# A planned three-stage kernel: attention in groups of three units, own maxima behind the scores

## The chip, the cores and the metric

The kernel runs on one core of one Trainium2 chip. The metric is the device time of one execution in microseconds; the time before is 989.42 us, the median of three runs (987.98, 989.42, 990.55).

## What is computed

Three stages, each on the output of the one before: an attention whose queries are averaged in twos, a dense feed-forward layer with ELU, and a soft mixture of experts. The change touches the first.

```python
def _attn_ref(q, k, v):                  # (4, 8, 1152, 64) each
    q_pool = q.reshape(B, H, S // 2, 2, D).mean(axis=3)
    scores = scale * np.matmul(q_pool, k.transpose(0, 1, 3, 2))
    scores = scores - np.max(scores, axis=-1, keepdims=True)
    attn = np.exp(scores)
    attn = attn / (np.sum(attn, axis=-1, keepdims=True) + 1e-09)
    return np.matmul(attn, v)

h = x @ w_in; g = np.where(h > 0, h, np.exp(np.minimum(h, 0)) - 1); x = g @ w_out
# then soft mixture of 8 experts with 4 slots each on the 2304 x 512 result
```

## The kernel before

**The attention.** The 32 heads are taken in 16 pairs. A pair has two halves of 288 pooled queries, and each half goes over nine chunks of 128 keys: 18 units a pair. A unit (`step`, L675) consists of the scores of both heads (`qk`, L688: eight matmuls of 288 columns, the two heads on the two halves of the array's rows), the exponential on ScalarE (L700), the running sum of P on GpSimd or DVE (L709), and P times V (`pv`, L695: two heads on the two halves of the array's columns). At the end of a half, the sums over the keys are formed on TensorE (`sums`, L719).

The row maximum must be known before a half begins, since its negative is added by the fourth product of `qk` (the operand `nm`). It is computed from single products of q and k (L619) and a reduction on DVE (L628). Six products of 384 columns per pair have a score tile of their own (`max_unit`, "own" maxima); eighteen of 192 columns are carried behind the scores of a unit of the pair before, in the free columns of the same tile (`carry`). `max_end` (L664, L668, L672) turns the maxima into a row.

q and k of a pair are transposed on TensorE (L580 for q, L603 for k: six blocks in a score tile and three in an accumulator), cast by ScalarE (L588, L610) and the rest of the cast is taken by a subtraction on DVE (L589, L611).

**Tiles.** Three score tiles of two PSUM banks each (psA twice, psS) serve scores, own maxima and transposes in turn; two accumulators (psC) serve P times V, sums, the row of the maxima and k's last three blocks. Six buffers hold P.

**What sets the order.** All operations are entered with a wished position, a duration and their operands, and a planner (`Plan.run`) lists them on the five engines by estimated times; the instructions are then issued in that order, engine by engine, and the semaphores follow from the tiles that they touch. TensorE's operations of the attention are fixed: they keep the order of their positions. Positions are written in groups of GU = 2 units (L569): scores of the group's units, then P times V of the group before.

```python
        t = TG(p, u // GU, 0.45 * (u % GU))
        t2 = TG(p, u // GU + 1, TC + 0.2 * (u % GU))
        ...
        if more:
            max_red(S_, *more, 1, NH, t + 0.02, [("SX", p, u)])
```

The last argument makes the planner put the reduction of a carried maximum behind the unit's exponential (`SX`).

The dense layer follows (L856, L895, 32 slots), with its weights decoded on DVE beside the attention and the layer itself, and the experts at the end (L1241, L1277), whose weights arrive as the buffers come free.

Of the kernel before, what the change touches and what calls it, by code (L numbers as in the profile page):

```python
# [270 lines left out]
DQ = [-10, 0.61]
DK = [[-9, 0.3], [-9, 0.3]]
UC = -14
MAX1 = [[-2, 0.4], [-2, 1.3], [0, -0.1], [0, 0.9], [1, -0.1], [1, 1.3]]
# [1112 lines left out]
```

## Time and profile before

| | |
|---|---|
| median of three runs | 989.42 us |
| span of the profiled execution | 990.1 us |
| TensorE matmuls busy | 955.2 us, 96% |
| VectorE busy | 757.0 us, 76% |
| ScalarE busy | 497.7 us, 50% |
| GpSimd busy | 396.2 us, 40% |
| mean granted clock of TensorE | 0.980 |
| chain that ended last | TensorE 85%, VectorE 8%, DMA 3% |

The profiled execution's span lies within the range of the three runs, 0.7 us above their median; there is no other time for it. The attention takes about the first half of the span, the dense layer the time up to some 908 us, the experts the rest. GpSimd is busy in the attention alone. A busy TensorE row includes its pipeline: consecutive rows overlap, so durations on TensorE are read from start to start.

### The profile page before, as it was taken

To read this page: it belongs to the slowest core of one execution; us is meant where nothing else is said; L and a number is where in the kernel's file an instruction comes from. 1 tells how busy PE (TensorE), PEld (TensorE's weight loads), DVE (VectorE), ACT (ScalarE), POOL (GpSimd) and SP (SyncE) were. 2 spreads that over 40 slices of the span, in tenths; PEclk is the share of its full clock that TensorE was granted. 3 is DMA by queue.
4 is the path that set the end of the run, shared out by engine and by line. 5 is a ranking of instruction groups with operands and counts; after the bars stand their busy time and mean duration, and the time that the engine had idled before them with its cause. 6 is when DMAs were issued, how large, how long until landed. Compare 5 with 4: busy or idle time off the path is not lost.

```text
span 990.1 us, 20893 instructions
## 1 busy us (share of the span) xinstructions
PE 955.2 (96%) x8474; PEld 782.5 (79%) x8474; DVE 757.0 (76%) x1278; ACT 497.7 (50%) x891; POOL 396.2 (40%) x278
## 2 busy tenths in 40 slices
PE   7999999999999999999999999999999999999885
PEld 4777767676777677677899999999999999998343
DVE  6677788888777778899998989998866877766213
ACT  2556566555665556565664444444434376442213
POOL 2878889798878878887400000000000000001000
PEclk7999999999999999999999999999999999999897
DMA  7133424224334322221263333333423023233999
GB/s 177 45 86 85 106 74 122 67 78 119 86 85 117 74 73 75 63 72 34 65 219 113 117 95 131 106 98 110 157 86 107 32 97 107 65 107 109 402 362 317
DMA packets 103663, 114.86 MB, mean 116 GB/s; under 512 B 43664, under 2 KB 74896, under 8 KB 103568
## 3 DMA queue, kind: packets, MB, share of 16 engines
q1 hardware_dynamic: 103568, 113.55, 37.7%
q8 instruction: 66, 1.08, 0.5%
q14 instruction: 29, 0.24, 0.1%
HBM read 100.27 MB, written 13.18 MB: 115 GB/s over the span
## 4 chain that ended last, share of the span: by engine, by line
PE 85%; DVE 8%; DMA 3%; ACT 1%; issue 1%; SPq 0%; ACTq 0%; DVEq 0%
PE psC L895 20%; PE psA L856 20%; PE psC L695 13%; PE psA L688 10%; PE psS L688 5%; PE psA L619 3%; PE psS L619 2%; DVE memf L628 2%; DMA memzq<-in_moe_w_dram 2%; PE psA L1241 2%; PE psC L719 1%; PE psA L603 1%; DMA memf<-memf 1%; PE psA L580 1%; PE psC L664 1%; PE psC L1277 1%
## 5 line engine op out<-in xcount | busy, mean ns | idle before, releaser
L709 POOL TENSOR_TENSOR memf<-memf 128x576 f32<-128x576 f32 x241 | 359.8, 1495 | 65.0 <-ACT memf L700 38.6
L895 PE MATMUL psC<-memz 128*128 128x288 f32 x1512 | 224.6, 296 | 1.2 <-DVE memf L906 0.7
L895 PEld LDWEIGHTS psC<-memz 128*128 128x128 f32 x1512 | 208.1, 188 | 4.6 <-ACT memf L514 1.6
L695 PE MATMUL psC<-memf 128*64 128x288 f32 x1152 | 174.6, 420 | 0.0
L700 ACT ACTIVATE memf<-psA 128x576 f32<-128x576 f32 x206 | 132.8, 651 | 66.8 <-PE psA L619 57.7
L628 DVE TENSOR_REDUCE memf<-psA 128x2 f32<-128x384 f32 (+3 forms) x235 | 142.4, 617 | 28.7 <-PE psA L619 13.9
L1347 POOL MEMSET memf<- 128x2048 f32 x1 | 1.8, 1817 | 387.8 <-DVE memz L517 387.8
L906 DVE TENSOR_TENSOR memf<-psC,memf 128x288 f32<-128x288 f32 x220 | 100.3, 462 | 47.4 <-PE psC L895 45.6
L628 DVE TENSOR_REDUCE memf<-psS 128x4 f32<-128x768 f32 (+1 forms) x140 | 103.5, 739 | 38.1 <-PE psS L619 21.2
L514 ACT CAST memz<-memf 128x576 fp32r<-128x576 f32 (+1 forms) x94 | 69.2, 749 | 82.6 <-PE psC L895 42.1
L695 PEld LDWEIGHTS psC<-memf 128*64 128x64 f32 x1152 | 70.0, 136 | 48.9 <-issue 9.9
L517 DVE TENSOR_TENSOR memz<-memf,memz 128x576 fp32r<-128x576 f32 (+1 forms) x108 | 96.9, 906 | 9.8 <-ACT memz L514 8.6
L856 PE MATMUL psA<-memz 128*128 128x288 f32 x512 | 93.8, 295 | 0.0
L867 ACT ACTIVATE memf<-psA 128x576 f32<-128x576 f32 x64 | 41.7, 652 | 103.3 <-PE psA L856 103.2
L688 PE MATMUL psA<-memr 64*128 64x288 f32 x816 | 73.3, 303 | 3.9 <-DVE memf L628 3.9
L856 PEld LDWEIGHTS psA<-memz 128*128 128x128 f32 x512 | 76.6, 188 | 0.0
L700 ACT ACTIVATE memf<-psS 128x576 f32<-128x576 f32 x82 | 53.4, 651 | 41.0 <-PE psS L619 36.1
L688 PEld LDWEIGHTS psA<-memr 64*128 64x128 f32 x816 | 60.1, 188 | 11.0 <-DVE memf L628 6.1
L688 PE MATMUL psA<-memy 64*128 64x288 f32 x624 | 61.3, 301 | 0.5 <-DVE memf L628 0.4
L856 PE MATMUL psA<-memz,memv 128*128 128x288 f32 x256 | 51.9, 296 | 0.0
L688 PEld LDWEIGHTS psA<-memy 64*128 64x128 f32 x624 | 47.3, 187 | 4.5 <-issue 3.5
L870 DVE SCALAR_TENSOR_TENSOR memf<-memf,psA 128x576 f32<-128x576 f32 x64 | 47.6, 744 | 1.7 <-ACT memf L868 1.6
(210 smaller groups left out, 1512.6 us busy)
## 6 DMA issues: line engine op xcount, KB each, us to landing
memf<-wscr SPq DMA_DIRECT2D x32, 512.0 KB
memzq<-in_moe_w_dram SPq DMA_DIRECT2D x30, 512.0 KB
memf<-in_moe_w_dram SPq DMA_DIRECT2D x26, 512.0 KB
memz<-in_q_dram SPq DMA_DIRECT2D x32, 288.0 KB
memz<-in_k_dram SPq DMA_DIRECT2D x32, 288.0 KB
memf<-in_v_dram SPq DMA_DIRECT2D x16, 576.0 KB
memf<-in_moe_w_in_dram SPq DMA_DIRECT2D x32, 256.0 KB
wscr<-memf SPq DMA_DIRECT2D x32, 256.0 KB
```

The lines of the kernel that those rows point to most:

```text
L514: return lambda e: nc.scalar.copy(out_, in_) if e == "ACT" else nc.vector.tensor_copy(out_, in_)
L517: return lambda e: ENG[e].tensor_tensor(out_, a, b, ALU.subtract)
L619: nc.tensor.matmul(tile_[:m, j, lo : lo + n * MW], lhsT=qkb["qh", i][js, o : o + m], rhs=qkb["kh", i][js, g * MW : (g + n) * MW], start=Tr ...
L628: add(t, "DVE", dve(2 * n * MW), lambda: nc.vector.reduce_max(MX[i][:m, a, :, g : g + n], v4(got(psS, tok)[:m, :, lo : lo + n * MW], n), a ...
L688: nc.tensor.matmul(sp[:, j, :NH], lhsT=qkb[w, i][js, cs] if w else ONER[js], rhs=qkb[m, i][js, hs], start=(x == 0), stop=(x == 3))
L695: nc.tensor.matmul(psC[h][j * D : (j + 1) * D, :NH], lhsT=VR[i][:, j, c], rhs=e[:, j], start=(c == 0), stop=(c == NC - 1))
L700: add(t + 0.01, "ACT", act(NQ, True), lambda: nc.scalar.activation(got(EAf, E_), got(psS, S_)[:, :, :NH], AF.Exp, scale=1.0 / 16.0), r=[S_ ...
L709: ENG[e].tensor_tensor(ac, a, got(EAf, E_), ALU.add)
L856: nc.tensor.matmul(ph[:, t, :NH], lhsT=a, rhs=x, start=(i == 0), stop=(i == 3 * KD - 1))
L870: add(t + 1.2, "DVE", dve(NQ), lambda: nc.vector.scalar_tensor_tensor(got(Ef, uk), got(Uf, ek), -1.0, ph(), ALU.add, ALU.max), r=[ek, A], ...
L895: nc.tensor.matmul(po_(), lhsT=a, rhs=x, start=(i == 0), stop=(i == 3 * GF - 1))
L906: add(t0 + 0.8, "DVE", dve(NH), lambda: nc.vector.tensor_tensor(d, po_(), d, ALU.add), r=[ck], w=XK)
```

## The change

Groups are listed in GS, six of three units per pair, and GB holds each group's first unit. Positions count groups through `TG`; `TP` stands in the middle of a group. P times V of a unit comes LAG = 1 unit later than its scores' group allows: the first two units of a group in that group, the third in the next. Own maxima get positions of 1.6 (behind a group's scores). The reduction of a carried maximum no longer waits for the exponential in the planner's list. The transposes get new positions, and the planner's durations, priorities (PRI) and biases new numbers, of which two lines stand for all.

```diff
 def pool(n):
-    return n * 0.00229 + 0.11
+    return n * 0.00229 + 0.17
-SWITCH = 0.18
+SWITCH = 0.195
-PRI = {'1AtaPE': -5.3608, ...
+PRI = {'1AtaPE': -5.3608, ...
-GU = 2
+GS = [3, 3, 3, 3, 3, 3]
+GB = [sum(GS[:i]) for i in range(len(GS))]
+LAG = 1
-DQ = [-10, 0.61]
-DK = [[-9, 0.3], [-9, 0.3]]
-UC = -14
+DQ = [-6, 0.983]
+DK = [[-6, 1.6683], [-6, 0.7]]
+UC = -15
-MAX2 = [[[-7, 0.4], [-6, -0.1], [-5, -0.1], [-4, -0.1]], [[-2, -0.1], [-1, -0.1]]]
+MAX2 = [[[-5, 1.6], [-4, 2.9408], [-3, 1.6], [-2, 1.6]], [[-1, 1.6], [0, -0.9777]]]
...
     def TG(p, d, x):
-        return (NU * p + GU * d) * STEP + x
-
-    TC = 0.5 * GU * STEP
+        return (NU * (p + d // len(GS)) + GB[d % len(GS)]) * STEP + x
+
+    def TP(p, d, x):
+        return TG(p, d, 0.5 * GS[d % len(GS)] * STEP + x)
...
-        t = TG(p, u // GU, 0.45 * (u % GU))
-        t2 = TG(p, u // GU + 1, TC + 0.2 * (u % GU))
+        g = max(x for x in range(len(GS)) if GB[x] <= u)
+        t = TG(p, g, 0.45 * (u - GB[g]))
+        g2 = g + (u - GB[g] >= GS[g] - LAG)
+        t2 = TP(p, g2, 0.2 * (u - GB[g] - (GS[g] if g2 > g else 0)) + 0.2 * LAG)
...
         if more:
-            max_red(S_, *more, 1, NH, t + 0.02, [("SX", p, u)])
+            max_red(S_, *more, 1, NH, t + 0.02)
...
-            t3 = TG(p, u // GU + 1 + SUMD[h][0], TC + SUMD[h][1])
+            t3 = TP(p, g2 + SUMD[h][0], SUMD[h][1])
...
-        prep_q(p, TG(p, DQ[0], TC + DQ[1]))
+        prep_q(p, TP(p, DQ[0], DQ[1]))
         for g in range(2):
-            prep_k(p, g, TG(p, DK[g][0] if p else (-9 if GU == 2 else -6), TC + DK[g][1] + 0.01 * g))
+            prep_k(p, g, TP(p, DK[g][0], DK[g][1] + 0.01 * g))
```

Lines of the changed kernel are five further on in the attention: L622 is the product for maxima (L619 before), L693 the scores (L688), L700 P times V (L695), L724 the sums (L719), L631 the reduction (L628), L705 the exponential (L700), L583 and L606 the transposes (L580, L603), L614 and L592 the subtractions (L611, L589).

One group on TensorE before, in the middle of a pair. psA_78, psA_79 and psS_85 are the three score tiles, psC an accumulator; 384 columns are an own maximum, 192 a carried one.

```order
L619 MATMUL psS_85<-memy 128x384 x2
L688 MATMUL psA_78<-memr 128x288 x8
L619 MATMUL psA_78<-memy 128x192 x2
L688 MATMUL psA_79<-memr 128x288 x8
L619 MATMUL psA_79<-memy 128x192 x2
L695 MATMUL psC_80<-memf 64x288 x4
```

One group on TensorE in the change, and the first scores of the next:

```order
L693 MATMUL psA_78<-memr 128x288 x8
L622 MATMUL psA_78<-memy 128x192 x2
L693 MATMUL psA_79<-memr 128x288 x8
L622 MATMUL psA_79<-memy 128x192 x2
L693 MATMUL psS_85<-memr 128x288 x8
L622 MATMUL psS_85<-memy 128x192 x2
L622 MATMUL psA_78<-memy 128x384 x2
L700 MATMUL psC_80<-memf 64x288 x2
L700 MATMUL psC_81<-memf 64x288 x4
L693 MATMUL psA_79<-memr 128x288 x8
```

The own maximum stood ahead of the scores, in the tile that the group's scores don't use; it stands behind them now, in the tile of the group's first scores, with P times V behind it.

DVE in the change in another such group (its first unit is in psS_85), with the engines that its instructions wait for: the reductions of three carried maxima, of the own one behind them, and of the own one that opens the next group (both two by two).

```order
L631 TENSOR_REDUCE memf<-psS_85 64x2 [waits Activation_49]
L631 TENSOR_REDUCE memf<-psA_78 64x2 [waits PE_49]
L631 TENSOR_REDUCE memf<-psA_79 128x2 [waits PE_49]
L631 TENSOR_REDUCE memf<-psS_85 128x2x2 [waits PE_49]
L631 TENSOR_REDUCE memf<-psA_78 128x2x2 [waits PE_49,Activation_49]
```

The first reduction stands behind ScalarE's exponential on the same tile; where a reduction waits for TensorE alone, the exponential of that tile stands behind the reduction.

The transposes of the next pair on TensorE before: q's between two groups, k's between the next two.

```order
L695 MATMUL psC_81<-memf 64x288 x4
L580 MATMUL psA_79<-ident,memf 128x96 x6
L688 MATMUL psS_85<-memy 128x288 x6
L688 MATMUL psS_85<-memy,memr 128x288 x2
L619 MATMUL psS_85<-memy 128x192 x2
L688 MATMUL psA_78<-memy 128x288 x6
L688 MATMUL psA_78<-memy,memr 128x288 x2
L619 MATMUL psA_78<-memy 128x192 x2
L695 MATMUL psC_81<-memf 64x288 x4
L603 MATMUL psA_79<-ident,memz_96 128x128 x6
L603 MATMUL psC_81<-ident,memz_96 128x128 x3
```

And in the change, with the group behind them:

```order
L700 MATMUL psC_80<-memf 64x288 x4
L606 MATMUL psC_81<-ident,memz_96 128x128 x3
L583 MATMUL psS_85<-ident,memf 128x96 x6
L606 MATMUL psA_78<-ident,memz_96 128x128 x6
L693 MATMUL psA_79<-memr 128x288 x8
L622 MATMUL psA_79<-memy 128x192 x2
L693 MATMUL psS_85<-memr 128x288 x8
L622 MATMUL psS_85<-memy 128x192 x2
L693 MATMUL psA_78<-memr 128x288 x8
```

All fifteen blocks stand together now, and the second and third scores behind them use the tiles of q's and k's transposes.

## Rows read from the trace of the kernel before

**Rows 1.** Busy time and share of the span, by engine, from the page.

```profile
PE 955.2 (96%) x8474; PEld 782.5 (79%) x8474; DVE 757.0 (76%) x1278; ACT 497.7 (50%) x891; POOL 396.2 (40%) x278
```

**Rows 2.** Busy by stretch (length, five engines, clock, DMA): two of thirteen periods, sum.

```profile
134.30:161.90 27.60, 27.60 (x295) 19.87 (x293) 24.10 (x36) 16.54 (x29) 23.34 (x16) 1.00 0.38 106
...
331.10:362.20 31.10, 29.43 (x296) 21.15 (x294) 21.76 (x36) 16.55 (x29) 23.44 (x17) 0.95 0.31 68
...
sum 367.90, PE 362.78 PEld 259.73 DVE 291.87 ACT 218.45 POOL 310.94; mean PE 27.91 PEld 19.98 DVE 22.45 ACT 16.80 POOL 23.92
```

**Rows 3.** Timeline of TensorE, two groups: start us, us, engine, line, operation, tiles, count.

```profile
206.24 0.44 PE L619 MATMUL psS<-memr 64*128 64x384 f32 x2
206.52 0.58 PE L688 MATMUL psA<-memy 64*128 64x288 f32 x6
...
207.08 0.25 PE L619 MATMUL psA<-memr 64*128 64x192 f32 x2
207.17 0.57 PE L688 MATMUL psA<-memy 64*128 64x288 f32 x6
...
207.72 0.25 PE L619 MATMUL psA<-memr 64*128 64x192 f32 x2
207.90 1.19 PE L695 MATMUL psC<-memf 128*64 128x288 f32 x8
209.02 0.67 PE L688 MATMUL psS<-memy 64*128 64x288 f32 x6
...
209.66 0.25 PE L619 MATMUL psS<-memr 64*128 64x192 f32 x2
...
477.33 1.68 PE L695 MATMUL psC<-memf 128*64 128x288 f32 x12
478.94 0.40 PE L856 MATMUL psA<-memz,memv 128*128 128x288 f32 x1
```

**Rows 4.** Timeline of ScalarE and DVE in the first of those groups.

```profile
207.42 1.29 ACT L700 ACTIVATE memf<-psA 128x576 f32<-128x576 f32 x2 [1.49 <-PE psA L619]
...
208.11 1.19 DVE L628 TENSOR_REDUCE memf<-psA 128x2 f32<-128x384 f32 x2 [0.39 <-ACT memf L700]
```

**Rows 5.** Timeline around scores that waited for DVE, at 128 us.

```profile
128.07 0.55 DVE L628 TENSOR_REDUCE memf<-psS 128x2 f32<-128x384 f32 x1
...
128.67 0.80 PE L688 MATMUL psS<-memr 64*128 64x288 f32 x8 [0.63 <-DVE memf L628]
129.30 0.25 PE L619 MATMUL psS<-memy 64*64 64x192 f32 x2
```

**Rows 6.** Timeline around the transposes of one pair.

```profile
218.67 0.72 PE L580 MATMUL psA<-ident,memf 96*128 96x96 f32 x6
...
219.32 0.80 PE L688 MATMUL psS<-memr 64*128 64x288 f32 x8
...
220.10 0.76 DVE L589 TENSOR_TENSOR memy<-psA,memy 128x576 fp32r<-128x576 f32 x1 [0.60 <-ACT memy L588]
...
221.90 0.87 PE L603 MATMUL psA<-ident,memz 128*128 128x128 f32 x6
...
222.49 1.97 DVE L709 TENSOR_TENSOR memf<-memf 128x576 f32<-128x576 f32 x1
222.61 0.49 PE L603 MATMUL psC<-ident,memz 128*128 128x128 f32 x3
222.81 0.80 ACT L610 CAST memy<-psA 128x768 fp32r<-128x768 f32 x1 [0.40 <-PE psA L603]
...
224.38 0.94 DVE L611 TENSOR_TENSOR memy<-psA,memy 128x768 fp32r<-128x768 f32 x1
```

**Rows 7.** Timeline of DVE at 345 us.

```profile
345.42 0.54 DVE L744 RECIPROCAL memf<-memf 18x64 f32<-18x64 f32 x1 [2.41 <-DMA memf<-memf]
```

**Rows 8.** Timeline of the last scalings before the output is stored.

```profile
979.36 2.60 DVE L1315 TENSOR_TENSOR memzq<-psB,memf 128x512 f32<-128x512 f32 x4 [0.60 <-PE psB L1308]
...
982.37 0.84 ACT L1313 ACTIVATE memzq<-psB,memf 128x256 f32<-128x256 f32 x2 [0.48 <-PE psB L1308]
```

More of the change, by code (lines that the diff above doesn't have):

```diff
@@ L254 @@
+BIAS = [{'DVE': 0.5175, 'Pool': -0.5461, 'ACT': -0.3368}, {'DVE': -2.7428, 'Pool': 5.8552, 'ACT': -4.78}, {'DVE': 11.7028, 'Pool': 29.6502, 'ACT': 12.3672}, {'ACT': -12.7593, 'Pool': 2.7731, 'DVE': 0.0167}]
 LOOK = {'PE': 0.0215, 'ACT': 0.293, 'DVE': 0.1477, 'Pool': 0.3598, 'SP': 5.2367}
 STEP = 1.47
-GU = 2
+GS = [3, 3, 3, 3, 3, 3]
+GB = [sum(GS[:i]) for i in range(len(GS))]
+LAG = 1
 NDEC = [0, 0, 0, 0, 1, 0, 1, 1, 0, 0, 0, 0, 1, 0, 0, 1]
@@ L270 @@
 OGRP = [[2, 6, 12, 18], [6, 12, 16, 18]]
[L271 to L278 removed]
+DQ = [-6, 0.983]
+DK = [[-6, 1.6683], [-6, 0.7]]
+UC = -15
+MAX1 = [[-2, 0.2327], [1, 1.3], [0, 0.239], [-1, -0.0374], [0, 1.1719], [0, -0.1]]
+DE1 = [[-1, 0.6], [2, -0.0791]]
+MAX2 = [[[-5, 1.6], [-4, 2.9408], [-3, 1.6], [-2, 1.6]], [[-1, 1.6], [0, -0.9777]]]
+DE = [[-1, -0.05], [2, -0.2464]]
+SUMD = [[1, 0.1772], [1, 0.3]]
 MOE0 = 1.422
@@ L643, in attention_moe_softmoe @@
         if p == 0:
-            own[p] = [(a, g, *((-7 + x // 2, 0.2 * (x % 2)) if GU == 2 else (-5 + x // 3, 0.2 * (x % 3)))) for x, (a, g) in enumerate(cells[0])]
+            own[p] = [(a, g, -5 + x // 3, 0.2 * (x % 3)) for x, (a, g) in enumerate(cells[0])]
             own[p] += [(a, g, *MAX1[x]) for x, (a, g) in enumerate(cells[1])]
@@ L695, in pv @@
                 nc.tensor.matmul(psC[h][j * D : (j + 1) * D, :NH], lhsT=VR[i][:, j, c], rhs=e[:, j], start=(c == 0), stop=(c == NC - 1))
-        g = 0 if c < 6 else 1
+        kg = 0 if c < 6 else 1
         more = carry.get((p, u))
-        add(t, "PE", 0.6 if more else 0.512, qk, r=(max_deps(more[0], more[2], 1) if more else []) + [("qh", i), ("ql", i), ("kh", i, g), ("kl", i, g), ("nm", i, h, 0), ("nm", i, h, 1), ("ONER", 0)], w=[S_], mode="R", fixed=True)
+        add(t, "PE", 0.617 if more else 0.53, qk, r=(max_deps(more[0], more[2], 1) if more else []) + [("qh", i), ("ql", i), ("kh", i, kg), ("kl", i, kg), ("nm", i, h, 0), ("nm", i, h, 1), ("ONER", 0)], w=[S_], mode="R", fixed=True)
         add(t + 0.01, "ACT", act(NQ, True), lambda: nc.scalar.activation(
@@ L711, in step @@
             add(t + 1.0, ("DVE", "Pool"), (dve(NQ), pool(NQ)), acc, r=[E_] + ([("EA", p, u - 1)] if c == 1 else []), w=[ak], port=True)
-        add(t2, "PE", 0.476, pv, r=[E_, ("VR", i)], w=[("C", h)], mode="C", fixed=True)
+        add(t2, "PE", 0.482, pv, r=[E_, ("VR", i)], w=[("C", h)], mode="C", fixed=True)
         if c == NC - 1:
             add(t2 + 0.01, ("ACT", "DVE"), (act(NH, True), dve(NH)), lambda e: copy_(UA[i][:, h], psC[h][:, :NH])(e), r=[("C", h)], w=[("UA", i, h)])
-            t3 = TG(p, u // GU + 1 + SUMD[h][0], TC + SUMD[h][1])
+            t3 = TP(p, g2 + SUMD[h][0], SUMD[h][1])
             def sums():
@@ L719, in sums @@
                     nc.tensor.matmul(psC[h][j * D : (j + 1) * D, :NH], lhsT=ONEF, rhs=ac[:, j], start=True, stop=True)
-            add(t3, "PE", 0.476, sums, r=[ak, ("ONEF", 0)], w=[("C", h)], mode="C", fixed=True)
+            add(t3, "PE", 0.482, sums, r=[ak, ("ONEF", 0)], w=[("C", h)], mode="C", fixed=True)
             add(t3 + 0.01, "ACT", act(NH, True), lambda: nc.scalar.activation(
```

12 lines of the change are left out of this document (4 added, 8 removed).

## The prediction

> **What bounds the kernel now.** I read the busy shares first: TensorE is busy for 96% of the span [rows 1], so the question is how long the program keeps it occupied and where it stands. Then I cut the attention part into its periods, one per head pair, from one transpose of q to the next [rows 2]. A period in which TensorE waits for nothing takes 27.60 us; the thirteen periods shown by the sum row take 367.9 us, so 367.9 - 13 x 27.6 = 9.1 us of waiting lie in them, 3.5 us of it in one period. VectorE is busy 24.1 us of the 27.6 and GpSimd 23.3 us in that period: both are close, neither is the bound. Last I read TensorE's own timeline start to start [rows 3], because the ends of its rows overlap, and the ACT and DVE rows beside it [rows 4].
>
> **Term 1: fewer changes between scores and P times V.** The scores use half the rows of the array per head (L688, L619), P times V and its like half the columns (L695). In [rows 3], P times V for two units takes 1.12 us to the next start (207.90 to 209.02), for three units 1.61 us (477.33 to 478.94). Six units so cost 3 x 1.12 = 3.36 us now and 2 x 1.61 = 3.22 us in threes. Ahead of it the carried maximum takes 0.18 us (207.72 to 207.90) instead of the 0.09 us that it takes ahead of scores (207.08 to 207.17), and the first scores behind it 0.64 us (209.02 to 209.66) instead of 0.55 us (207.17 to 207.72). One group fewer is worth 0.14 + 0.09 + 0.09 = 0.32 us. A pair goes from nine groups to six, sixteen pairs make 48 groups: **-15.4 us**. Moving the own maxima behind the scores changes this by nothing: ahead of them one takes 0.28 us (206.24 to 206.52), of which the change of mode is a part that the first scores pay then.
>
> **Term 2: a score tile comes free too late for the own maximum.** There are three score tiles. Now a group uses own, scores, scores, then P times V, so a tile is used again 2.75 us later or more. In the change a group fills all three with scores and the own maximum follows at once in the tile of the group's first unit. What that tile must do first is told by four rows. The carried maximum starts 0.64 us after the scores, the exponential 0.34 us after that (207.08, 207.42) and lasts 0.65 us (half of the 1.29 for two); the reduction of the carried maximum starts 0.04 us after the exponential's end (207.42 + 0.65, then 208.11) [rows 3, 4], lasts 0.55 us, and TensorE goes on 0.05 us after its end (128.07 + 0.55, then 128.67) [rows 5]. Sum 2.27 us. The own maximum stands 0.64 + 0.09 + 0.55 + 0.09 + 0.55 + 0.09 = 2.01 us behind the scores' start. It waits 0.26 us, and the scores after such a wait took 0.63 us (128.67 to 129.30) instead of 0.56 us (206.52 to 207.08) [rows 3, 5], so 0.33 us in all. Behind that own maximum stand P times V and the whole next group. Four of the six own maxima of a pair stand so; the one in the group behind the transposes is covered by the wait of term 3. Three in fifteen pairs make 45 x 0.33 = **+14.9 us**. No row of the kernel before shows this turn itself; the bounds are 0 (the turn fits) and 0.5 us (a reduction that comes a little late as well), so 0 to 22 us. I take the sum of the four rows because each of them repeats through the whole trace.
>
> The change takes the dependency on the exponential out of the planner's list for the carried maximum, so the planner may believe that both read the tile at once. In the built order of the change the reduction still waits for ScalarE, or the exponential for the reduction; either way the tile is free after one and the other. Against this change speaks a rule of the Trainium skill, PSUM — Partial Sum Buffer, section PSUM bank collisions raise a hardware error: two engines that touch the same bank and quadrant are kept apart, reads against reads included. By that rule the 2.27 us stand; without it the reduction would hide under the exponential, the turn would be 0.64 + 0.34 + 0.65 + 0.05 = 1.68 us, and term 2 would be nothing. The trace agrees with the rule in the row at 208.11, where the idle reduction starts only when the exponential has ended.
>
> **Term 3: the transposes in one place.** Now q's stand between two groups and k's between the next two [rows 6], and two of the three tiles serve the scores meanwhile. In the change the nine of k and six of q follow each other, take two tiles, and the group behind them wants all three. q's tile: transposes at 218.67, the subtraction on it ends at 220.10 + 0.76, so 2.24 us with the 0.05 us to TensorE. In the change q's take about 0.57 us (0.65 less the 0.08 of the change of mode that its row contains), k's six 0.79 us (222.61 - 221.90 plus that 0.08), the first unit 0.73 us: the second unit stands 2.09 us behind and waits 0.15 us. k's tile: cast 0.91 us after the transposes' start and 0.80 us long, then 0.04 + 0.94 + 0.05 us, 2.74 us; the third unit stands 0.79 + 0.73 + 0.15 + 0.64 = 2.31 us behind and waits 0.43 us. With 0.07 us lost after each wait 0.72 us, in fifteen pairs **+10.8 us**. At the least it is the 0.43 us alone (6.5 us). At the most a sum of P (1.97 us at 222.49) or a decoding step stands ahead of the subtractions on DVE's queue, as in most later pairs of the new order; DVE is idle there by my count for about a microsecond, so up to 1 us more in ten pairs, 21 us.
>
> **Term 4: the waits that are there.** The 9.1 us of [rows 2] come from DVE arriving late at a reduction (0.63 us in [rows 5]) and, in one period, from a reciprocal that stood 2.41 us for its transfer with the reductions behind it [rows 7]. The DVE work is nearly the same afterwards: 22 sums of P instead of 15, and ten of the q sums instead of thirteen. The order is new, the tiles' turns are shorter. I take half of it away, **-4.5 us**, between all of it (-9.1) and none.
>
> **Term 5: the rest.** The MoE part has the same TensorE work, and follows the attention as before. At the very end DVE scales seven of the last nine blocks instead of five: 979.36 + 7 x 0.65 = 983.9, where now ScalarE's last ends at 982.37 + 0.84 = 983.2 [rows 8]: **+0.7 us**. GpSimd does 234 sums instead of 241, three more sums of q, one more normalisation and one decoding step fewer: no change against its 23.3 us of 27.6. The first pair's transposes of q move behind k's arrival; I leave it at 0, within 1 us either way. P times V of a group's first two units now follows in the same group. Where DVE reduces the second unit's carried maximum before ScalarE takes its exponential, that exponential ends at about 1.67 + 0.46 + 0.55 + 0.05 + 0.65 = 3.4 us into the group, and its P times V stands at 2.27 + 0.28 + 2 x 0.5 = 3.55 us: hidden, by little, and 0.3 us a group if DVE is late.
>
> **Sum**: -15.4 + 14.9 + 10.8 - 4.5 + 0.7 = +6.5 us, so 996.6 us by the profiled execution's span of 990.1. That execution stands 0.7 us above the median, 989.42; from the median the forecast is 995.9 us. A measurement of this kernel can tell about 0.3%, 3 us, from no change: 986.5 to 992.4 would be the same.
>
> **The rivals.**
> Faster: the turn of a score tile fits into the group, because exponential and reduction lie closer than in [rows 4]. It decides at one number: a turn of 2.01 us or less. Then term 2 is 0 and the sum is -15.4 + 10.8 - 4.5 + 0.7 = -8.4, 981.0 us. For it speaks that ScalarE and VectorE have idle time in each group; against it that each piece of the turn has its row. By the rule of the page above this rival would not come about: 0.21.
> The same: the wait is there but smaller, 0.2 us each (9 us instead of 14.9): 990.0 us. A few of the pieces measured overlap by some hundredths, so 0.17.
> Slower still: with no slack left in the tiles' turns, every late arrival of DVE goes straight into TensorE. All waits of before stay (+4.5) and another 0.5 us per pair comes on top (+7.5): 1007.9 us. The seven additional sums on DVE speak for it, the 3.5 us of idle DVE per period against it: 0.12.
> The change not doing what it says would show in the order: groups are of three there, and four of six own maxima stand behind a group's scores, two behind P times V. That is not open.
>
> **The numbers.** Forecast 0.50, rivals 0.21, 0.17 and 0.12. The forecast's own range, with term 2 from 9 to 20 and term 3 from 6.5 to 14, is 990 to 1003. The range for all is 981.5 to 1004: it leaves out about half of the fastest rival and most of the slowest. Faster by over 0.3%: 0.21; within: the third case and a little of the forecast, 0.18; slower: 0.61.
>
> **What would show it.** Periods of the attention of about 28.7 us instead of 28.3 in the mean; the own maxima (L622) waiting for DVE's reductions (L631) some 45 times by 0.2 to 0.4 us, and scores behind the transposes waiting for the subtractions (L614) about 15 times by 0.4 us; 96 starts of P times V in threes at 1.61 us. Periods near 27 us without waits of the own maxima would prove term 2 wrong. Waits spread over all score rows, with DVE busy through, would mean the third rival.

## The result, and the profile after

The change made the kernel slower: 1001.36 us, the median of four runs (999.90 to 1003.01), against 989.98 us for the kernel before (four runs, 987.98 to 991.53). The ratio is 1.0113, with a 95% interval of 1.0092 to 1.0134, so 11.4 us more. The profiled execution of the change has a span of 999.6 us against 990.1 us: it shows 9.5 of these 11.4 us. Two lines of its page, the busy time and the chain that ended last, answer to [rows 1] and to the table ahead of them:

```profile
PE 957.8 (96%) x8474; PEld 784.6 (78%) x8474; DVE 765.5 (77%) x1307; ACT 484.9 (49%) x862; POOL 389.5 (39%) x274
...
PE 77%; DVE 11%; ACT 6%; DMA 3%; issue 2%; POOL 0%; SPq 0%; ACTq 0%; DVEq 0%; POOLq 0%
```

TensorE is hardly busier (957.8 us for 955.2), yet its share of the chain falls from 85% to 77%, and ScalarE's goes from 1% to 6%, DVE's from 8% to 11%: the chain now runs through an exponential and a reduction at many places where TensorE stands.

Where the 9.5 us lie, by stretches: start and first pair up to the first scores of the second pair; pairs 1 to 14 from first scores to first scores; the last pair with the dense layer; the experts. Busy time by stretch, the kernel before first (the columns are those of [rows 2]):

```profile
0.00:50.37 50.37, 42.83 (x353) 29.77 (x353) 33.92 (x51) 20.17 (x35) 27.52 (x31) 0.86 0.48 109
50.37:445.90 395.53, 390.21 (x4098) 279.06 (x4098) 317.43 (x490) 237.10 (x417) 334.80 (x228) 1.00 0.34 87
445.90:908.41 462.51, 458.54 (x3488) 443.15 (x3487) 385.50 (x675) 219.08 (x375) 33.88 (x21) 1.00 0.30 100
908.41:990.10 81.69, 63.62 (x543) 30.55 (x541) 20.15 (x63) 21.35 (x66) 0.00 (x0) 0.86 1.00 354
```

The same stretches of the change, and behind them the shortest of its pairs:

```profile
0.00:50.59 50.59, 42.62 (x353) 29.07 (x355) 32.84 (x51) 19.71 (x35) 27.35 (x31) 0.90 0.51 109
50.59:456.35 405.76, 394.96 (x4106) 282.04 (x4106) 322.19 (x500) 232.16 (x417) 331.11 (x225) 1.00 0.31 84
456.35:915.85 459.50, 456.08 (x3483) 442.39 (x3481) 380.30 (x663) 221.95 (x380) 31.00 (x20) 1.00 0.30 101
915.85:999.60 83.75, 64.16 (x543) 31.12 (x541) 30.20 (x94) 11.08 (x31) 0.00 (x0) 0.86 0.98 345
...
397.02:425.50 28.48, 28.11 (x297) 20.25 (x296) 24.23 (x37) 16.64 (x30) 23.02 (x16) 1.00 0.28 81
```

The differences are +0.2, +10.2, -3.0 and +2.1 us. Pairs 1 to 14 decide. Their time splits in two. The shortest pair I take for one that nothing irregular delays, and call it the undisturbed period: 27.60 us before [rows 2], 28.48 us now. Fourteen of them are 386.4 us before and 398.7 us now; what is left of the stretch, 9.1 and 7.0 us, I call the disturbances. The change lengthens every period by 0.88 us and has slightly fewer disturbances.

**The steady waits.** One group of the change, TensorE, ScalarE and DVE (columns as in [rows 3, 4]):

```profile
210.49 0.56 PE L693 MATMUL psA<-memy 64*128 64x288 f32 x6
...
211.40 1.29 ACT L705 ACTIVATE memf<-psA 128x576 f32<-128x576 f32 x2 [0.63 <-POOL memf L714]
...
212.08 1.20 DVE L631 TENSOR_REDUCE memf<-psA 128x2 f32<-128x384 f32 x2 [0.42 <-ACT memf L705]
...
212.35 0.25 PE L622 MATMUL psS<-memr 64*128 64x192 f32 x2
...
212.69 0.45 PE L622 MATMUL psA<-memr 64*128 64x384 f32 x2
213.07 1.68 PE L700 MATMUL psC<-memf 128*64 128x288 f32 x12
```

The first unit's scores start at 210.49, its exponential at 211.40, its reduction at 212.08, and the own maximum (384 columns, the same tile) at 212.69. The tile's turn is 2.20 us; in the two other places of a pair where an own maximum waits it is 2.27 to 2.29 us nearly throughout. The own maximum stands 0.34 us behind the carried one instead of 0.09 us, and P times V 0.38 us behind it, 0.09 to 0.10 us more than where nothing waited. The list of waits has only three of these places, because the modelled end of the row ahead covers it; start to start shows it. Of the 60 own maxima that follow a carried one, 36 stand 0.30 us or more behind it. The 15 of them that come behind the transposes are not among the 36.

Behind the transposes:

```profile
257.68 0.66 PE L583 MATMUL psA<-ident,memf 96*128 96x96 f32 x6
258.17 0.82 PE L606 MATMUL psA<-ident,memz 128*128 128x128 f32 x6
...
258.92 0.66 PE L693 MATMUL psS<-memy 64*128 64x288 f32 x6
259.03 0.80 ACT L613 CAST memr<-psA 128x768 fp32r<-128x768 f32 x1
...
259.86 0.96 DVE L614 TENSOR_TENSOR memr<-psA,memr 128x768 fp32r<-128x768 f32 x1
259.88 0.35 PE L622 MATMUL psS<-memr 64*128 64x192 f32 x2 [0.16 <-ACT memr L613]
260.07 0.59 PE L693 MATMUL psA<-memy 64*128 64x288 f32 x6
...
260.63 0.25 PE L622 MATMUL psA<-memr 64*128 64x192 f32 x2
260.88 0.67 PE L693 MATMUL psA<-memy 64*128 64x288 f32 x6
```

The first wait is not at a score tile. The carried maximum of the first unit is a product of the new k, whose cast ends at 259.83: the maximum starts 0.96 us behind its scores instead of 0.63 us. The second and third scores then wait 0.10 and 0.16 us for the tiles of the transposes.

**The end.** The last stretches of the experts, from the last weights' arrival on; first the kernel before, then the change:

```profile
976.10:978.50 2.40, 1.31 (x10) 0.40 (x10) 0.16 (x1) 0.74 (x2) 0.00 (x0) 1.00 1.09 387
978.50:983.30 4.80, 3.44 (x18) 2.67 (x18) 3.54 (x6) 3.13 (x8) 0.00 (x0) 0.80 0.78 272
```

```profile
984.40:988.00 3.60, 1.99 (x11) 0.77 (x12) 1.27 (x3) 0.00 (x0) 0.00 (x0) 0.68 1.01 352
988.00:993.50 5.50, 4.32 (x18) 3.73 (x18) 4.46 (x7) 1.68 (x4) 0.00 (x0) 0.50 0.51 173
```

From the last products on the last weights to the end it is 14.0 us before (from 976.10) and 15.2 us now (from 984.38). The granted clock is 0.50, the lower of its two levels (1.2 GHz), in the last 5.5 us of TensorE's and DVE's work now (to 993.50) and 0.80 in the stretch that answers to it, and DVE does more of the scalings (4.46 us for 3.54). The other 0.8 us lie ahead of the last weights.

### The profile page after: what moved, and what is told of

It is laid out like the page before. It is cut to its first block, busy times and chain, and to the rows that moved or that the text cites. A ratio compares the mean times of both kernels' runs of the same rounds, so it can differ in the third digit from the quotient of the medians.

```text
span 999.6 us, 20814 instructions
## 1 busy us (share of the span) xinstructions
PE 957.8 (96%) x8474; PEld 784.6 (78%) x8474; DVE 765.5 (77%) x1307; ACT 484.9 (49%) x862; POOL 389.5 (39%) x274
## 4 chain that ended last, share of the span: by engine, by line
PE 77%; DVE 11%; ACT 6%; DMA 3%; issue 2%; POOL 0%; SPq 0%; ACTq 0%; DVEq 0%; POOLq 0%
PE psA L861 20%; PE psC L900 20%; PE psC L700 12%; PE psA L693 7%; DVE memf L631 6%; ACT memf L705 4%; PE psS L693 3%; PE psA L622 3%; DMA memzq<-in_moe_w_dram 2%; PE psS L622 2%; PE psC L724 1%; PE psA L1246 1%; DVE memz L519 1%; PE psC L1282 1%; PE psB L1052 1%
## 5 line engine op out<-in xcount | busy, mean ns | idle before, releaser
L714 POOL TENSOR_TENSOR memf<-memf 128x576 f32<-128x576 f32 x234 | 350.1, 1498 | 89.3 <-ACT memf L705 47.2
L631 DVE TENSOR_REDUCE memf<-psA 128x4 f32<-128x768 f32 (+2 forms) x251 | 161.1, 661 | 55.9 <-ACT memf L705 44.3
L705 ACT ACTIVATE memf<-psA 128x576 f32<-128x576 f32 x190 | 121.5, 651 | 112.0 <-PE psA L622 65.7
L700 PE MATMUL psC<-memf 128*64 128x288 f32 x1152 | 167.0, 415 | 0.0
L700 PEld LDWEIGHTS psC<-memf 128*64 128x64 f32 x1152 | 73.6, 136 | 52.3 <-issue 11.9
L516 ACT CAST memz<-memf 128x576 fp32r<-128x576 f32 (+1 forms) x101 | 74.5, 751 | 68.8 <-DVE memf L875 51.4
L631 DVE TENSOR_REDUCE memf<-psS 128x2 f32<-128x384 f32 (+2 forms) x124 | 81.7, 659 | 30.4 <-ACT memf L705 22.5
L872 ACT ACTIVATE memf<-psA 128x576 f32<-128x576 f32 x64 | 41.8, 653 | 117.1 <-PE psA L861 114.3
L705 ACT ACTIVATE memf<-psS 128x576 f32<-128x576 f32 x98 | 63.8, 651 | 53.7 <-PE psS L622 31.1
L693 PE MATMUL psA<-memr 64*128 64x288 f32 x760 | 68.9, 304 | 1.3 <-DVE memf L631 1.2
L693 PEld LDWEIGHTS psA<-memr 64*128 64x128 f32 x760 | 54.2, 185 | 11.9 <-issue 5.5
L693 PE MATMUL psA<-memy 64*128 64x288 f32 x570 | 58.7, 311 | 1.7 <-DVE memf L631 1.2
L693 PEld LDWEIGHTS psA<-memy 64*128 64x128 f32 x570 | 42.1, 187 | 11.8 <-issue 5.0
```

The source lines that it names most:

```text
L516: return lambda e: nc.scalar.copy(out_, in_) if e == "ACT" else nc.vector.tensor_copy(out_, in_)
L631: add(t, "DVE", dve(2 * n * MW), lambda: nc.vector.reduce_max(MX[i][:m, a, :, g : g + n], v4(got(psS, tok)[:m, :, lo : lo + n * MW], n), a ...
L693: nc.tensor.matmul(sp[:, j, :NH], lhsT=qkb[w, i][js, cs] if w else ONER[js], rhs=qkb[m, i][js, hs], start=(x == 0), stop=(x == 3))
L700: nc.tensor.matmul(psC[h][j * D : (j + 1) * D, :NH], lhsT=VR[i][:, j, c], rhs=e[:, j], start=(c == 0), stop=(c == NC - 1))
L705: add(t + 0.01, "ACT", act(NQ, True), lambda: nc.scalar.activation(got(EAf, E_), got(psS, S_)[:, :, :NH], AF.Exp, scale=1.0 / 16.0), r=[S_ ...
L714: ENG[e].tensor_tensor(ac, a, got(EAf, E_), ALU.add)
```

## The experiments

Twelve kernels. For each the total is given, its ratio to the kernel before run beside it (whose medians lay between 988.1 and 990.2 us), and the undisturbed period, which is the shortest from a pair's first scores to the next pair's, and the disturbances, which are pairs 1 to 14 less fourteen such periods:

| kernel | total, us | ratio to before (95%) | undisturbed period | disturbances |
|---|---|---|---|---|
| before | 989.3 | | 27.60 | 9.1 |
| the change | 1001.4 | 1.0113 (1.0092 to 1.0134) | 28.48 | 7.0 |
| own maxima behind P times V | 1033.3 | 1.0440 (1.0422 to 1.0458) | 29.14 | 22.3 |
| k's last blocks behind | 997.6 | 1.0086 (1.0072 to 1.0100) | 28.34 | 7.3 |
| both | 1028.1 | 1.0394 (1.0373 to 1.0415) | 28.81 | 31.0 |
| before, own maxima behind the scores | 992.6 | 1.0034 (1.0021 to 1.0046) | 27.70 | 9.2 |
| mixed groups | 1005.3 | 1.0164 (1.0143 to 1.0185) | 27.22 | 15.8 |
| first carried maximum left out | 998.7 | 1.0094 (1.0069 to 1.0119) | 26.74 | 19.9 |
| third carried maximum left out | 1011.1 | 1.0225 (1.0206 to 1.0244) | 28.19 | 12.1 |
| planner's old numbers | 1015.1 | 1.0256 (1.0235 to 1.0277) | 28.41 | 13.5 |
| mixed, refitted | 988.7 | 0.9992 (0.9977 to 1.0006) | 27.25 | 12.6 |
| mixed, refitted again | 992.4 | 1.0028 (1.0016 to 1.0040) | 27.53 | 9.1 |
| reduction behind the exponential | 1024.4 | 1.0345 (1.0318 to 1.0371) | 28.39 | 22.4 |
| mixed, fitted with slack | 991.4 | 1.0012 (0.9997 to 1.0027) | 27.25 | 10.3 |

The table is the finding of the study. The undisturbed period came out within about 0.2 us of what the reasons said in nine of the twelve kernels. In the two with own maxima behind P times V a wait that nobody had counted came on top, and in one of the mixed kernels it was 0.25 us too long. The totals mostly did not follow, because every edit also gives the planner another list, and the disturbances then lie anywhere from 7 to 31 us.

### First round: where the own maxima and the transposes stand

**Own maxima behind P times V.**

```diff
-MAX2 = [[[-5, 1.6], [-4, 2.9408], [-3, 1.6], [-2, 1.6]], [[-1, 1.6], [0, -0.9777]]]
+MAX2 = [[[-5, 2.94], [-4, 2.9408], [-3, 2.94], [-2, 2.94]], [[-1, 2.94], [0, 2.85]]]
```

> The changed kernel with one line other: the own maxima stand behind P times V of their group instead of behind its scores (groups of three, LAG and the transposes as in the change). Theory A (the score tile's turn of 2.27 us against 2.01 us): behind P times V the tile has 1.6 us more, so the steady waits of 0.25 us and what follows each (0.09 us) go in three places per pair. 3 x 15 x 0.35 = 15.7 us less than the changed kernel's 1001.4, so 985.7 us (983 to 989), and faster than the kernel before. The own maximum's tile is then wanted by the third scores 1.56 us later, and its reduction takes about 1.5 us with what stands around it, so a few small waits may appear there. Theory B (DVE is late whatever the place, with 22.7 us of 28.9 busy): the waits follow the reductions to the third scores; 997 to 1003 us. Theory C (three units in a group cost by themselves, in the change between scores and P times V): no change, 1001.

It took 1033.3 us, a plain miss: 48 us above the expectation, slower than the change by 32 us. The largest wait of TensorE in total over pairs 1 to 14 is a new one (columns: engine, tile, line, what it waited for; us in total, times, longest):

```profile
PE psC L667 <- DVE memv L671: 22.1, 14, 1.6
PE psA L693 <- DVE memf L631: 6.4, 12, 1.2
PE psS L693 <- DVE memf L631: 5.5, 6, 2.3
```

and its place, with DVE's queue:

```profile
228.77 0.55 DVE L631 TENSOR_REDUCE memf<-psS 64x2 f32<-64x384 f32 x1 [0.39 <-ACT memf L705]
...
229.38 0.55 DVE L631 TENSOR_REDUCE memf<-psA 64x2 f32<-64x384 f32 x1
230.10 0.56 DVE L631 TENSOR_REDUCE memf<-psA 128x2 f32<-128x384 f32 x1 [0.17 <-ACT memf L705]
230.57 0.18 DVE L671 TENSOR_REDUCE memv<-memf 128x6 fp32r<-128x36 f32 x1
...
230.90 0.33 PE L667 MATMUL psC<-memv 128*64 128x128 f32 x3 [1.58 <-DVE memv L671]
```

The row of the maxima (L667), which stands between scores and P times V, waits 1.6 us in every pair: with the own maxima later, the planner put the small reduction ahead of the row (L671) behind three reductions of carried maxima, each of which waits for its exponential. I had moved six own maxima and had not asked what is queued between the last of them and the row. The waits of the own maxima are gone: the scores behind an own maximum follow it after 0.28 us, as where nothing waits. The undisturbed period is 29.14 us, and without the wait of the row it would be 29.14 - 1.6 = 27.5 us: 1.0 us less than the change's 28.48 us, as the 3 x 0.35 us of theory A say. So the term fits in size and the edit loses for another reason; its disturbances are 22.3 us on top.

**k's last three blocks behind the other transposes.**

```diff
-DK = [[-6, 1.6683], [-6, 0.7]]
+DK = [[-6, 1.6683], [-6, 1.8]]
```

> The changed kernel with one number other: the three blocks of k that go into an accumulator are transposed behind the twelve others instead of ahead of them, so that q's six and k's six start 0.38 us earlier against the scores behind them. Theory A (the scores and the carried maximum behind the transposes wait for fixed chains of cast and subtraction, 2.24 us for q's tile and 2.74 us for k's): k's tile is then ready 0.57 + 2.74 = 3.31 us behind the start, the third scores stand at 0.57 + 0.75 + 0.38 + 0.63 + 0.64 = 2.97 us, so 0.34 us of wait and 0.09 us behind it are left of 0.78 us per pair: 15 x 0.35 = 5.2 us less, 996 us (994 to 998). Theory B (DVE is busy with a sum of P or a decoding step when the subtraction's turn comes): the place of three blocks on TensorE changes nothing, 1000 to 1002. Theory C (one wait takes another's place, since ScalarE now casts k's last three blocks between the exponentials): 1001 to 1004.

997.6 us: 8.3 us above the kernel before beside it (ratio 1.0086), where the change was 11.4 us above its own, so about 3 us less where 5.2 were expected. The rows behind the transposes tell why:

```profile
229.17 0.80 PE L693 MATMUL psA<-memr 64*128 64x288 f32 x8
...
229.80 0.36 PE L622 MATMUL psA<-memy 64*128 64x192 f32 x2
230.00 0.71 PE L693 MATMUL psA<-memr 64*128 64x288 f32 x8
...
231.42 0.26 PE L622 MATMUL psS<-memy 64*128 64x192 f32 x2
...
231.72 0.44 PE L622 MATMUL psA<-memy 64*128 64x384 f32 x2
```

The carried maximum no longer waits (0.63 us behind its scores), but the own maximum at the end of this group now does: 0.30 us behind the carried one instead of 0.09 us. In the change the waits behind the transposes had covered it. The prediction had counted this own maximum as covered, and the expectation forgot that the cover goes with the wait. Of 0.34 us spared about 0.2 are given back; the period falls from 28.48 to 28.34 us. Theory A has the mechanism right and its size too large by that.

**Both edits.** The own maxima and k's blocks as in the two diffs.

> Both edits at once: own maxima behind P times V, and k's last three blocks behind the other transposes. Theory A: the two savings lie in different places of a pair and add up, 1001.4 - 15.7 - 5.2 = 980.5 us (977 to 985), 0.9% faster than the kernel before; what is left above the time without waits is then DVE's late arrivals. Theory B (DVE late whatever the place): no better than the kernel before, 988 to 1000.

1028.1 us, a miss again, with the new wait of the row; nothing adds up where one of the two edits disturbs the list.

**The kernel before with own maxima behind the scores.**

```diff
-MAX2 = [[[-7, 0.4], [-6, -0.1], [-5, -0.1], [-4, -0.1]], [[-2, -0.1], [-1, -0.1]]]
+MAX2 = [[[-7, 0.7], [-6, 0.7], [-5, 0.7], [-4, 0.7]], [[-2, 0.7], [-1, 0.7]]]
```

> The kernel before (groups of two) with one line other: the own maxima stand behind a group's scores instead of ahead of them, as in the change. Theory A: with two scores on three tiles the own maximum takes the third tile, which its group does not use, so nothing waits: 988 to 992 us, no change against the kernel before's 989.98. Theory B (the place behind the scores costs by itself, through the change of mode or because DVE has the carried maxima ahead of it): 0.35 us in each of some 90 places, 31 us, so about 1020; half of them, 1005.

992.6 us, 3.3 us (0.34%) slower, just outside theory A's range and far from theory B's. The period is 27.70 for 27.60 us. In groups of two, where the third tile is free, the place behind the scores costs next to nothing; what costs is that place in a group that fills all three tiles.

### Second round: the tile's turn against DVE's load

**Leaving out a third of the carried maxima**, once that of each group's first unit, once that of its third.

```diff
+    for x in [x for x in carry if x[1] % 3 == 0]:
+        del carry[x]
```

and with 2 in place of 0 in the other. Both spare DVE and TensorE the same, on TensorE 6 x 0.09 us a pair; only the first shortens the turn of the tile that the own maximum takes.

> The changed kernel without the carried maximum of each group's first unit: a third of the carried products and of their reductions is left out, the row maximum is taken over the rest. TensorE is spared 6 x 0.09 us a pair, DVE 6 x 0.55 us. Theory A (the turn of the first unit's tile): without the reduction the turn is 0.55 + 0.34 + 0.65 + 0.05 = 1.6 us, the own maximum stands 1.9 us behind, so the steady waits go: 1001.4 - 15 x 0.54 - 15 x 1.05 = 977.6 us (974 to 983). Theory B (DVE's load): the same as the next kernel, which spares DVE as much, within 3 us.

> The changed kernel without the carried maximum of each group's third unit: as much is left out as in the kernel above, but the turn of the first unit's tile stays at 2.27 us while the own maximum comes 0.09 us sooner. Theory A: the waits of the own maxima stay, or grow by the 0.09 us spared ahead of them: 1001.4 - 15 x (0.54 - 0.27) to - 15 x 0.54, 993 to 998 us. Theory B (DVE's load): 975 to 985 us, as the kernel above.

Early pairs of both, one after the other, in which little else is on DVE:

```profile
49.21:75.99 26.78, 26.61 (x283) 19.29 (x283) 14.98 (x24) 16.10 (x29) 24.59 (x18) 1.00 0.30 80
```

```profile
52.34:80.92 28.58, 27.84 (x283) 19.41 (x283) 15.14 (x24) 15.90 (x29) 25.05 (x19) 1.00 0.28 75
```

DVE is busy 14.98 and 15.14 us, the same; the periods are 26.78 and 28.58 us. The change's own early pair takes 28.62 us:

```profile
50.59:79.21 28.62, 28.16 (x297) 20.05 (x295) 17.70 (x30) 16.00 (x29) 25.04 (x19) 1.00 0.30 74
```

Leaving out work of DVE alone gives nearly nothing here (0.04 us; 0.29 us between the shortest pairs, which 0.54 us less of products on TensorE would cover). The kernel with the shorter turn gains 1.84 us: 0.54 us of it is the products, some 0.4 us lie behind the transposes, where the carried maximum that waited for k's cast is gone, and the rest, 0.9 us, is about what three waits of 0.35 us come to. Start to start the own maxima of this kernel stand 0.09 us behind the carried one in 52 of 60 places, as where nothing waits. This is the clearest of the twelve: the steady loss comes from the turn of the tile, not from DVE's load. In the second kernel the turn is what the prediction summed, 2.27 us, almost to the hundredth:

```profile
99.94 0.67 PE L695 MATMUL psS<-memy 64*128 64x288 f32 x6
...
100.92 0.65 ACT L707 ACTIVATE memf<-psS 128x576 f32<-128x576 f32 x1 [1.43 <-PE psS L622]
...
101.61 0.56 DVE L631 TENSOR_REDUCE memf<-psS 128x2 f32<-128x384 f32 x1 [2.19 <-ACT memf L707]
...
102.22 0.44 PE L622 MATMUL psS<-memr 64*128 64x384 f32 x2 [0.20 <-DVE memf L631]
```

From 99.94 to 102.22 it is 2.28 us: 0.98 to the exponential, 0.65 for it, 0.04 to the reduction, 0.56 for it, 0.05 to TensorE. The totals, 998.7 and 1011.1 us, are 21 us above theory A's figure for the first and 13 us above the top of its range for the second: the disturbances are 19.9 and 12.1 us where the change has 7.0, and the rest lies behind the attention.

**Mixed groups.** Six groups of two units, each with an own maximum ahead of its scores, and two groups of three without one.

```diff
-GS = [3, 3, 3, 3, 3, 3]
+GS = [3, 2, 2, 2, 2, 2, 2, 3]
-LAG = 1
+LAG = 2
-DQ = [-6, 0.983]
-DK = [[-6, 1.6683], [-6, 0.7]]
+DQ = [-8, 0.983]
+DK = [[-8, 1.6683], [-8, 1.8]]
-MAX2 = [[[-5, 1.6], [-4, 2.9408], [-3, 1.6], [-2, 1.6]], [[-1, 1.6], [0, -0.9777]]]
+MAX2 = [[[-6, -0.1], [-5, -0.1], [-4, -0.1], [-3, -0.1]], [[-2, -0.1], [-1, -0.1]]]
```

> The changed kernel's code with eight groups per pair: six of two units, each with an own maximum ahead of its scores in the third tile, and two of three units without one; the transposes stand behind the first group of three, k's last three blocks last, P times V again a whole group later for a group of two (LAG = 2). Theory A (what costs is that a group fills all three tiles and an own maximum or the transposes want a fourth): no tile is wanted before its turn is over. q's tile is ready 2.24 us behind its transposes and wanted after 2.33 us, k's after 3.31 us and wanted after 4.1 us. One group fewer than in the kernel before is worth 0.32 us a pair, the transposes in one place 0.08 us; the waits of the kernel before stay as they are: 989.5 - 15 x 0.40 = 983.5 us (981 to 988), faster than both. Theory B (the positions and the planner's numbers of the change make DVE late in any grouping): 992 to 1000. Theory C (e1's new wait): the row of the maxima stands 1.6 us late here too, 1005.

Two of its pairs:

```profile
78.14:105.36 27.22, 27.22 (x295) 19.94 (x293) 18.30 (x30) 16.17 (x29) 25.67 (x19) 1.00 0.30 77
...
188.21:219.69 31.48, 29.01 (x296) 21.31 (x294) 26.55 (x41) 16.77 (x30) 24.53 (x18) 0.95 0.25 67
```

The undisturbed period is 27.22 us, 0.38 us below the kernel before, where 0.40 us was expected, and TensorE is busy through all of it. Start to start, the scores follow every own maximum of this pair after 0.28 us, as where nothing waits: no tile makes an own maximum wait. The total is 1005.3 us all the same: 31.48 us in one pair, with the granted clock at 0.95 over it, and losses behind the last pair's first scores, of which the waits of TensorE show the longest:

```profile
PE psA L861 <- DVE memr L519: 3.4, 1, 3.4
```

That is the change to the dense layer, where the first decoded operands come late.

**The planner's old numbers.** PRI, BIAS, SWITCH and the durations of the kernel before in the change.

```diff
-SWITCH = 0.195
+SWITCH = 0.18
...
-PRI = {'1AtaPE': -5.3608, ...
+PRI = {'1AtaPE': -5.3608, ...
```

> The changed kernel with the planner's numbers of the kernel before (priorities, biases, durations, SWITCH); groups and positions as in the change. TensorE's order in the attention is fixed by positions, so the waits of the own maxima and behind the transposes stay. Theory A (the loss lies in groups and positions; the numbers decide the experts' end): the attention as in the change within 2 us, the end 1 to 2 us shorter: 999.5 us (997 to 1003). Theory B (the numbers made DVE late): 988 to 994. Theory C (the old numbers fit groups of two and order DVE worse here): 1004 to 1015.

1015.1 us, nearest to theory C: the period is 28.41 us, as the groups make it, but 13.5 us of disturbances and a later dense layer come on top. The change's own numbers are worth some 14 us against the old ones in this grouping. The experts' end is 83.7 us as in the change, so the 2.1 us there are not explained by these numbers.

### Third round: can the mixed groups be had without the disturbances?

Three times the mixed groups with the planner's numbers fitted anew (PRI, BIAS, LOOK, the offsets of the dense layer, the positions of the first pair, the rows and the sums), the third time with some slack in every duration. And the change with the planner's dependency put back:

```diff
-            max_red(S_, *more, 1, NH, t + 0.02)
+            max_red(S_, *more, 1, NH, t + 0.02, [("SX", p, u)])
```

> The mixed groups (six of two, two of three) again, with the planner's numbers (priorities, biases, offsets of the dense layer's steps, wished positions of the first pair and of the rows) fitted anew to this grouping by the planner's own list; TensorE's order within a pair as in the mixed kernel. Theory A (two separate things: the grouping sets the undisturbed period, the numbers set how often DVE and the change to the dense layer disturb it): the undisturbed period stays at 27.2 to 27.3 us against 27.6 us before, and the 16 us that the mixed kernel lost elsewhere go in the main: 984 to 993 us. Theory B (mixed groups themselves disturb DVE): 1000 to 1010 us again.

> The mixed groups with a second set of refitted numbers, started from the change's numbers where the kernel above started from those of the kernel before. Theory A as above: the same undisturbed period of 27.2 to 27.3 us, 984 to 997 us in all; the two kernels differ only in what lies outside undisturbed periods. Theory B: 1000 to 1010 us.

> The mixed groups once more, the planner's numbers now fitted so that the list holds also where ScalarE, DVE and GpSimd take some hundredths of a microsecond longer per instruction than planned. Theory A (what the mixed groups gain in the undisturbed period, 0.35 us a pair, was given back by DVE's late turns behind a list that fits only exact durations): fewer waits outside the undisturbed period of 27.2 to 27.3 us, 981 to 987 us, faster than the kernel before. Theory B (DVE's turns in the kernel before cannot be bettered by the list): 987 to 993 us, no change.

988.7, 992.4 and 991.4 us. The refitting took back 13 to 17 us of the mixed groups' loss, so that loss was the numbers' and not the grouping's. But none is measurably faster than the kernel before (0.9992, interval 0.9977 to 1.0006, at best): the 0.35 us per pair are there (27.25 us in the first and the third; 27.53 us in the second), and are given back in single pairs and, in the second and third, behind the attention. No kernel of this study beats both.

> The changed kernel with the kernel before's dependency put back: in the planner's list the reduction of a carried maximum stands behind the unit's exponential. Theory A (the built program keeps the two apart in any case, in one order or the other, and TensorE waits for the later of both): the steady waits of the own maxima and the undisturbed period of 28.5 us stay, 998 to 1006 us. Theory B (the removed dependency lets DVE go first and holds ScalarE and P times V back): 985 to 995 us.

1024.4 us with an undisturbed period of 28.39 us: the steady waits stay, as theory A said, but the list that follows from the old dependency has 22.4 us of disturbances. The removed dependency does nothing for the turn of a tile; it belongs to the numbers that were fitted with it.

What a disturbance is made of shows in the third of the mixed kernels, in its only long pair (31.93 us):

```profile
247.84 6.59 POOL L714 TENSOR_TENSOR memf<-memf 128x576 f32<-128x576 f32 x4
247.92 1.95 DVE L714 TENSOR_TENSOR memf<-memf 128x576 f32<-128x576 f32 x1
249.79 1.88 DVE L508 SCALAR_TENSOR_TENSOR memf<-memf 128x512 f32<-128x512 f32 x1
251.59 0.74 DVE L592 TENSOR_TENSOR memr<-psA,memr 128x576 fp32r<-128x576 f32 x1
...
252.39 0.85 PE L693 MATMUL psA<-memy 64*128 64x288 f32 x6 [2.83 <-DVE memr L592]
```

Two DVE instructions that take about 0.7 us each elsewhere take 1.95 and 1.88 us beside GpSimd's sums, the subtraction behind them comes 2.4 us late, and the scores stand 2.83 us for it. The longest wait of the kernel with the dependency put back, 2.76 us, stands behind two such instructions of L508 (3.72 us for both) beside GpSimd's sums.

## Why the prediction was right, and where it was off

The sign, the range and the mechanism of the largest term held: +6.5 us forecast, +11.4 us measured (9.5 us in the profile). Step by step:

- **Term 2 (score tile's turn), right.** Turns of 2.20 to 2.29 us were measured where 2.27 was summed, and 0.35 us lost at a wait where 0.33 was summed. Of the 45 places 36 show it in full; in seven others the third scores wait a little earlier, so that the own maximum behind them waits less. The pair of kernels with a third of the carried maxima left out excludes DVE's load as the cause of these waits.
- **Term 1 (fewer changes), right as far as it was tried.** It has no run of its own. In the trace of the change P times V of three units does take 1.61 us start to start, a carried maximum ahead of it 0.18 us, and the first scores behind it 0.63 us, within 0.01 us the prices that it was summed from. Taking the waits of terms 2 and 3 off the period, 28.48 - 1.05 - 0.67 = 26.76 us, leaves 0.84 us less than 27.60, for 0.96 forecast; in the mixed groups, one group fewer and the transposes in one place gave 0.35 to 0.38 us for 0.40.
- **Term 3 (transposes), right in sum, wrong in its parts.** 0.67 us a pair in the rows shown, 0.72 forecast. But half of it (0.33 us) is the first carried maximum waiting for k's cast, which the prediction did not have: it looked at the tiles that the scores take and not at the operand of the product behind them.
- **Term 4 (waits that were there), mis-sized.** I took half of 9.1 us away; 2.1 us went. And I read the 3.5 us of the long period in [rows 2] as waits alone: its clock is 0.95 and TensorE is busy 29.43 us in it instead of 27.60, so some 1.8 us of it are time at the lower clock and not waiting. The change has no such pair.
- **Term 5 (the end), mis-sized.** +0.7 forecast, +2.1 measured; the count of scalings was right, the granted clock of 0.50 in the last 5.5 us of work was not foreseen, and the 0.8 us ahead of the last weights have no cause shown. The last pair and the dense layer, which I had left at no change, gave 3.0 us back; which part of it is the last pair's groups I did not separate, so its cause stays open.

The terms of the period together: -0.96 + 0.99 + 0.72 = +0.75 us a pair forecast, +0.88 us measured. The miss of 3 us in the profile (5 in the medians) is made of 14 x 0.13 = 1.8 us there, 2.4 us in term 4 and 1.4 us at the end, less 2.6 us in the first pair, the last pair and the dense layer. That the total came so close owes something to luck: without this last part, which the prediction put at no change, the miss would be almost twice as large. The two faster or equal cases did not come about because the turn of the tile did not fit; the case of late DVE (third rival) did not either: disturbances fell from 9.1 to 7.0 us.

The rule of the Trainium skill that I leaned on (PSUM — Partial Sum Buffer, section PSUM bank collisions raise a hardware error: reads of two engines on one bank are kept apart) fits: in the rows at 100.92 and 101.61 the reduction starts 0.04 us behind the exponential's end. That the hardware itself needs it, no run here shows; the built programs order the two in every case. The row at 208.11, which the prediction gave for it, could not test it either, since in the kernel before the planner's list already puts the reduction behind the exponential.

## What to carry to other kernels

Count the buffers that a stretch between two long blocks of work wants, and set the turn of each (all its readers one after the other) against the time until it is wanted again: a larger group that wants one buffer more than there are pays at every group, whatever it saves in changes of mode. When an edit goes into a planned schedule, read the undisturbed period apart from the disturbances: the first tells whether the reason was right, and the total tells mostly whether the planner's numbers still fit.

## What the runs showed of the hardware that I had not expected

An instruction of DVE that reads two operands in SBUF is stretched when it begins while a GpSimd instruction runs. The sum of P (L714) takes 0.74 to 0.76 us in 21 of its 22 cases in the change, in which no GpSimd instruction runs beside it, and 1.98 us in the one where one does. In the kernel before three of fifteen begin inside a GpSimd instruction and take 1.97 to 1.98 us, one of them in [rows 6]; a fourth, which began 0.15 us ahead of one (at 210.04), took 0.75 us. I had read that 1.97 us as the price of a sum. The subtractions that read a score tile (L592) stayed at 0.74 to 0.76 us in all sixteen cases, fifteen of them beside GpSimd. The Trainium skill has this (SBUF — State Buffer, section SBUF: two separate sides: a DVE operation with two inputs in SBUF and a GpSimd operation that reads SBUF share a pair of ports, which the one that starts first holds for its whole instruction). The traces agree: the stretched sums end 0.6 us after the GpSimd instruction that they met. Not every overlap in the profile stretches DVE: in the third mixed kernel two decoding steps (L508, at 214.62 and 328.86) took 0.67 us beside a sum of GpSimd, and there that sum took 2.1 to 2.2 us instead of 1.4. In the two longest waits shown above this is what made DVE late: a sum or a decoding step that the planner puts into a short gap of DVE comes out a microsecond late, ahead of a subtraction or a reduction for which TensorE waits. How much of all disturbances it makes up, I did not count.

A wait is also paid twice: behind the 2.83 us in the third mixed kernel the granted clock fell to the lower level, 0.53 over the following stretch, so that TensorE's work there took longer:

```profile
248.00:252.70 4.70, 1.87 (x20) 1.46 (x20) 4.70 (x5) 2.17 (x4) 4.62 (x3) 1.00 0.34 126
252.70:256.30 3.60, 3.60 (x22) 1.91 (x18) 1.99 (x4) 0.65 (x1) 3.04 (x3) 0.53 1.01 234
```
